# A new list of steps for the first 720 steps of a delta-rule and feed-forward kernel

## The chip, the cores and the metric

One core of a Trainium2 chip runs the whole program. The metric is the device time in microseconds of one execution, the median of several. The engines are PE (TensorE, with PEld for its weight loads), DVE (VectorE), ACT (ScalarE), POOL (GpSimd) and SP (SyncE), which here issues nearly all transfers. Each engine works through its own instructions strictly in the order of the program.

## The reference

A delta-rule recurrence over 768 time steps, for 4 batches of 8 heads of 48 features, and a multiplicative feed-forward network on its output:

```
k_n = k / (norm(k) + 1e-6)
for t in range(S):
    y[t]  = q[t] @ state
    v_old = k_n[t] @ state
    state = state + beta[t] * outer(k_n[t], v[t] - v_old)
x   = y as (3072, 384)
out = (((x @ w1) * (x @ w2)) @ w3) @ w_out
```

w1 and w2 are 384x1024, w3 is 1024x1024, w_out 1024x384, all in float32.

## The kernel before

The 768 time steps are cut into 12 chunks of 64, and two chunks make one of 6 units. Within a chunk the recurrence becomes matrix products with the inverse of a triangular matrix, which is found for a unit (two chunks) at a time in blocks of 32; from chunk to chunk only the state goes on. w3 and w_out are multiplied with each other once (the fold), so that a unit's feed-forward part is two products of 384 by 1024, a multiplication, and one product of 1024 by 384, done with seven half-size products (a Strassen scheme).

Every piece of this is a Python generator, a *part*. A call of `step(name)` runs the part on to its next `yield` and so issues a few instructions. The text ORDER names 1317 steps, one word each; the kernel runs through it once, and `in_text_order()` (L128) then ties each engine to the order in which its instructions were recorded. So ORDER, written out by a planner offline, fixes the order on every engine and of the transfers on SP's queue. Nothing else schedules. A wait of one instruction holds up all that follow on its engine.

The parts that are spoken of below (m is a chunk, j a unit, and a part's steps are told by their place):

- `k`, `q`, `v`: loads of a chunk's keys, queries, values (L202, L213), by SP, those of chunk 0's k and q by ACT. `p`: eight loads of a chunk's keys, then eight of its queries, to be transposed (L230); `d`: DVE's four transposes of these (L324). `K0`, `Q0`, `K1`, `Q1`: the same for chunks 0 and 1 by PE (L337) and copies (L347, L349). `beta`: loads and transposes beta.
- `g`: the squares of the keys on POOL (L270), their sums on DVE (L272), a swap of halves by PE (L255). `N`: norms and weights from these, 15 short instructions on DVE (L279 to L303).
- `s`: a chunk's scores, twice: matmuls (L367, L373), a product on DVE into U (L379), and the masked P, for the first two chunks copied by ACT (L391) and masked by POOL (L393). `u`: four transfers of U to memory (L414).
- `V`: a unit's triangular inverse. POOL clears Vb (L422, L423), SP loads U as blocks (L426), ACT copies Vb to PSUM for the first two units (L434), DVE does 31 elimination steps of two instructions each (L440, L445), ACT copies back (L449), SP stores V (L453).
- `e`: a chunk's corner block: eight loads (L462, L469), a transpose on DVE (L481), matmuls (L498), ACT's copies (L514, L525). `n`: values times norms on POOL (L537).
- `c`: the chain of a chunk: products (L551), differences and scalings on DVE (L584, L594, L613, L615); it ends with the next state.
- `y`: a chunk's outputs: matmuls (L652), eight copies by ACT into xT (L673), and in the third step SP's transfers within xT (L684), six for each of chunks 0 and 1, six for two chunks later.
- `P0` to `P35`: pieces of weights. P0 to P7 are w_out (384 KB as loaded), P8 to P23 are w3 (512 KB), P24 to P29 are w1 and P30 to P35 are w2 (four loads each, 192 and 64 KB in turn). A piece is loaded into one of five raw buffers (L699), split by ACT (L707, L708), masked and joined by DVE (L710, L711), and added by POOL (L715), and only then its raw buffer is free for the load five pieces later.
- `t`: PE's transposes of a w3 piece (L750) and ACT's copy (L753); t0 to t15 belong to P8 to P23. `f`: the fold of a row block (L759, two halves; L766).
- `b`, `a`: unit 0's products with w1 and w2 for chunk 0 (`b`) and chunk 1 (`a0`), later whole units (`a1` and on): L779 on PE, ACT's copy (L791), DVE's multiplication (L795). The first half of each part uses w1, the second w2. They use four PSUM banks in turn.
- `T`, `S`, `o`, `x`: sums of the folded weights (L826), sums of slabs (L846), the seven products (L874), the result (L905 and on) and its transfers (L891).

PE has the same kind of work in every unit once it is under way; the beginning is different, since the weights must be loaded, rebuilt and folded, and the first inverse must be found, before the first product of unit 0 can start.

Of the kernel before, what the change touches and what calls it, by code (L numbers as in the profile page):

```python
# [36 lines left out]


ORDER = """
V0 P0 k0 beta P18 P13 P0 P18 P0 P0 P18 P18 g0 P11 beta P13 K0 K0 P11 P10 q0 P10 P3 k1 P11 P13  # L40
K0 beta P12 g0 P3 K0 g0 K0 g0 P13 K1 g0 P8 P12 g0 K1 K1 P11 P9 Q0 Q0 g0 Q0 P10 P12 g0 Q0 Q0 g0
k2 K1 s0 g0 P9 P10 P8 N0 K1 q1 P2 s0 N0 P3 Q1 s0 P12 p2 g1 Q1 P2 N0 s0 s0 Q1 P9 Q1 P8 Q1 g1 s0
P3 s0 t2 t2 t3 s1 P5 P8 P2 g1 s1 P2 P1 s1 s1 t3 P9 P5 s1 P4 s1 P5 u0 P5 s1 d2 P1 P4 t1 u1 t0 P6
t4 P7 t1 t10 P1 t0 t5 V0 t4 P14 g1 V0 P1 t10 P6 f1 t5 V0 d2 P4 P6 V0 V0 V0 P7 V0 P7 V0 P16 P14
V0 P4 V0 P19 P19 P19 P6 f0 P16 P17 P17 V0 V0 P16 V0 V0 P17 P7 f2 k3 P14 p2 V0 V0 v1 P19 P15 f1
f0 g1 f1 t11 V0 d2 t11 P15 f2 f5 V0 P14 P15 f0 P16 v0 P17 V0 V0 V0 V0 g1 P20 f5 V0 f2 f5 t6 t9
P15 t6 P20 t7 V0 n1 P22 P20 V0 t7 d2 s0 V0 V0 f3 P23 P20 P22 t8 P21 V0 n0 P24 n0 f3 V0 V0 n1 t8
V0 V0 t9 V0 V0 s2 p3 f4 f3 P23 P22 P26 g1 V0 g1 V0 f4 g1 P21 P22 P23 t14 d3 f4 P23 g1 t12 p3 V0
N1 P30 t12 t14 t15 e0 t15 d3 f7 d3 f6 e0 P30 P21 e0 e0 P24 f7 s2 s2 e1 e0 s2 P24 e0 e1 V1 p4 s2
e1 P26 s2 e1 P25 d3 c0 P21 P30 u2 s3 c0 s3 P26 N1 P31 P24 y0 s3 s3 y0 c0 s3 s3 P25 t13 N1 e1 u3  # L50
P31 c0 P26 P31 P32 c1 V1 c1 e1 P25 V1 P27 c1 V1 c1 V1 V1 t13 V1 V1 V1 V1 V1 V1 y0 V1 P25 f7 f6
f6 P30 P32 P32 v2 V1 P27 s1 P31 V1 V1 y1 b3 b1 V1 b0 P32 P28 y1 b1 V1 b1 b3 P29 P27 b2 b3 y1 V1
P27 b1 b0 P29 P29 c1 a01 b2 a03 P28 V1 a01 a00 b3 P28 P29 a02 a02 a03 P35 P28 V1 a05 b7 a00 V1
V1 V1 V1 a06 P33 V1 b5 a05 b7 b0 V1 P34 V1 b5 V1 a06 V1 V1 V1 P34 k4 V1 P35 V1 g2 a00 V1 k5 a00
b0 V1 V1 g2 a04 P34 n2 p4 n2 a07 c1 a04 b2 b4 P33 b6 b2 P35 V1 g2 g2 P34 g2 e2 a07 g2 P33 e2
P35 c2 c2 e3 d4 a03 d4 a03 a01 P33 g2 b4 d4 g2 e2 b6 e2 a07 e2 b4 d4 T a01 T b4 e2 a07 c2 s4 p5
g2 c2 T g2 N2 V2 b6 p5 b6 s4 b5 s4 c2 a06 c2 a06 a04 v3 y2 d5 b5 d5 k6 s4 e3 d5 s4 y2 a02 a05
d5 s4 b7 a04 n3 S0 a02 a05 S0 s5 S0 u4 e3 s5 n3 s5 e3 b7 T o0 c3 c3 s5 g3 s5 S0 N2 N2 x0 e3 g3
e3 o0 s5 c3 c3 u5 o0 x0 V2 S0 x0 y3 V2 y3 S0 V2 S0 V2 S0 S0 V2 V2 V2 S0 g3 o0 S0 o0 S0 x0 V2 c3
o0 v4 y3 V2 V2 V2 x0 p6 V2 x0 V2 S0 a10 a10 S0 g3 S0 x0 V2 x0 S0 o0 x0 x0 p6 a14 V2 k7 a17 a17  # L60
a14 V2 V2 V2 a15 a16 V2 a16 a15 V2 g3 V2 V2 V2 V2 V2 v5 V2 x0 a13 V2 V2 V2 a17 a12 V2 a13 g3 V2
V2 g3 a17 c3 a14 a13 d6 d6 a11 V2 e4 n4 a12 e4 e4 c4 d6 V3 e4 a14 a10 n4 g3 d6 c4 e5 a11 e4 s6
g3 a13 e4 a12 p7 a10 c4 g3 N3 s6 c4 s6 a11 y4 n5 y4 c4 e5 a12 c4 a11 a15 c5 n5 e5 p7 a16 d7 d7
d7 d7 o1 c5 v6 a16 k8 g4 g4 e5 g4 p8 a15 g4 s7 s7 S1 e5 s7 S1 e5 x1 s7 s7 S1 s7 c5 o1 s6 S1 u7
c5 o1 s6 s6 u6 S1 S1 V3 S1 y5 c5 c5 V3 V3 V3 V3 V3 o1 S1 x1 k9 S1 y5 S1 y5 o1 S1 S1 x1 x1 V3 S1
S1 V3 c6 V3 S1 S1 V3 d8 o1 x1 x1 v7 a20 n6 x1 V3 a20 o1 x1 a23 V3 V3 x1 V3 x1 n7 a27 a24 d8 a26
V3 V3 V3 V3 x1 g4 V3 a23 V3 a25 V3 a27 a27 V3 a24 V3 V3 a26 a20 V3 g4 V3 p8 V3 V3 V3 V3 p9 V3
V3 a25 d8 n6 d8 g4 a20 a22 a22 a24 V3 c6 a27 a25 a24 a21 a21 e6 e6 e6 g4 e7 N3 e6 a25 N3 g4 s8
g4 N4 s8 e6 a22 s8 a26 e6 c6 c6 N4 s8 a26 s8 y6 a22 V4 p9 N4 S2 d9 e7 s8 a21 e7 y6 u8 d9 a21 e7
c6 a23 d9 p10 e7 d9 S2 c6 S2 s9 n7 a23 s9 e7 o2 s9 c7 s9 S2 s9 k10 S2 c7 x2 o2 c7 S2 S2 o2 u9  # L70
s9 V4 c7 V4 S2 y7 V4 V4 x2 V4 g5 g5 V4 p10 d10 y7 S2 x2 S2 o2 y7 V4 o2 x2 c7 V4 V4 S2 S2 V4 o2
a35 x2 x2 k11 x2 S2 V4 x2 S2 a35 v8 V4 S2 V4 V4 S2 V4 x2 n8 o2 a37 x2 V4 v9 V4 V4 V4 x2 a34 n8
V4 V4 a36 a30 V4 V4 V4 V4 V4 a37 V4 a34 a33 V4 g5 a33 a30 a32 a36 V4 V4 V4 V4 a34 a33 V4 V5 a32
e8 n9 c7 e8 a30 c8 a33 e8 e9 e8 g5 a35 a34 c8 a30 e8 g5 d10 a32 e9 g5 a32 g5 a36 e8 e9 S3 c8
a36 a35 a31 d10 d10 e9 a31 n9 c8 g5 c8 c8 g5 g5 e9 a31 s10 N5 e9 p11 s10 s10 a31 c9 a37 a37 p11
c9 y8 N5 v11 d11 S3 d11 d11 o3 v10 d11 s10 y8 s10 S3 u10 S3 s11 N5 s11 o3 s10 c9 s11 c9 s11 S3
x3 S3 s11 o3 S3 S3 y9 o3 s11 x3 S3 o3 u11 V5 S3 S3 V5 y9 V5 x3 n11 S3 x3 V5 V5 V5 S3 y9 S3 S3
V5 c9 V5 o3 x3 V5 x3 x3 V5 V5 x3 S3 a47 o3 x3 V5 V5 a47 x3 V5 V5 a47 n10 V5 a46 a40 a40 V5 a47
V5 a43 V5 a46 x3 a42 a45 V5 a42 V5 a41 a45 a43 V5 V5 V5 V5 V5 V5 a44 V5 a44 V5 a45 a41 V5 V5 V5
V5 c9 a42 e10 a40 e10 n11 a42 e10 a44 e10 c10 a45 n10 e11 e10 e11 c10 a43 e10 c10 c10 a40 e11  # L80
a41 a46 e11 c10 a44 S4 a43 e11 a41 S4 c10 o4 e11 a46 c11 x4 S4 S4 y10 o4 c11 c11 S4 y10 S4 S4
S4 S4 S4 c11 o4 y11 o4 x4 S4 S4 S4 o4 y11 x4 x4 o4 S4 x4 x4 S4 y11 S4 x4 x4 a50 x4 o4 a50 x4
a55 a56 a55 a52 a55 a50 a52 a56 a54 a57 a54 a55 a54 a50 a54 a51 a52 a57 a51 a53 x4 a52 a53 a51
a56 a56 a53 a51 a53 a57 o5 S5 a57 S5 S5 o5 S5 S5 S5 x5 S5 S5 S5 o5 o5 x5 S5 S5 S5 o5 S5 S5 S5
o5 x5 S5 x5 o5 x5 x5 x5 x5 x5 x5 x5 x5 x5 x5
"""


# [1 line left out]
def kernel(  # L90
# [36 lines left out]
    def half(z):  # L127
        return slice(C * z, C * z + C)  # L128

    def feat(z):  # L130
        return slice(C * z, C * z + D)
# [6 lines left out]
    def in_turn(pool, shape, tag, n, name, dt=FP32):  # L138

        i = turns.get(tag, -1)  # L140
        while True:
            i = turns[tag] = (i + 1) % n
            if (tag, i) not in held:
                return pool.tile(shape, dt, tag=f"{tag}{i}", name=name, bufs=1)
# [14 lines left out]
    def in_text_order():  # L159
# [15 lines left out]
        out=strict[:], in_=strict[:], pattern=[[1, P]], compare_op=ALU.is_gt,  # L175
# [7 lines left out]
    def padded(name, shape, n, start=0):  # L183
        res = []
        for i in range(n):
            t = persist.tile(shape, FP32, name=f"{name}{i}")
            pool.memset(t[:, start:] if start else t[:], 0.0)
            res.append(t)
        return res

    TTs = padded("TT", [P, NR, H, C], 2)
# [3 lines left out]
    ktoks, vtoks, KQs, PTs, Xs, Ss = {}, {}, {}, {}, {}, {}  # L195
# [114 lines left out]
    def scale_of(x, m, crossed=0):  # L310
        j, cc = divmod(m, 2)
        return x[j][:, cc] if x is ns else x[j][:, crossed, cc]
# [219 lines left out]
    xts = {}  # L532

    def scaled_v(c):
        nv = vtoks[c]
        for r in range(NR):
            pool.tensor_tensor(  # L537
                out=nv[:, r], in0=nv[:, r],
                in1=scale_of(ns, c)[:, r].unsqueeze(2).to_broadcast([P, H, D]), op=ALU.mult,
            )  # L540
            yield

    def chain(c):
        TT, nv, KQ = TTs[c % 2], vtoks[c], KQs[c]

        def products(out, lhs, rhs):
            ps = two_banks()
            for r in range(NR):
                for h in range(H):
                    for z in range(2):  # L550
                        pe.matmul(  # L551
                            out(ps, r, h, z), lhsT=lhs(r, h, z), rhs=rhs(r, h, z),
                            start=True, stop=True,
                        )
            return ps[:, :, 0:DM].rearrange("p b (g d) -> p b g d", d=D)
# [15 lines left out]
            return St[feat(h % 2), z, NP * r + h // 2, :]  # L571

        St = Ss.get(c)
        R = nv
        if c > 0:
            ps = products(
                by_tokens_of_features, lambda r, h, z: KQ[feat(h % 2), NR * z + r, h // 2, 0, :], state
            )
            yield
            R = in_turn(work, [P, NR, H, D], "R", 1, "R")  # L580
            v3, r3 = (
                x[:].rearrange("p r (a e) d -> p (r a) e d", e=2) for x in (nv, R)
            )
            dve.tensor_tensor(  # L584
                out=r3, in0=v3, in1=ps.rearrange("p e g d -> p g e d"), op=ALU.subtract
            )
            yield
        ps = products(
            crossed, lambda r, h, z: TT[half(z), r, h, :], lambda r, h, z: R[half(z), r, h, :]
        )  # L590
        yield
        Xs[c] = X = in_turn(work, [P, NR, H, D], "X", 2, "X")
        for e in range(2):
            dve.tensor_tensor(  # L594
                out=X[:].rearrange("p r (a e) d -> p e (r a) d", e=2)[:, e], in0=ps[:, e],
# [449 lines left out]
```

## Time and profile before

| What | us |
|---|---|
| median of 3 runs | 598.36 |
| the three runs | 594.04, 598.36, 599.14 |
| the profiled execution, its own time | 593.18 |
| its span, first to last instruction | 591.5 |
| mean granted TensorE clock in it | 0.976 |
| L779, products with w1 and w2, busy | 128.0 + 131.8 |
| L874, the seven products, busy | 66.3 + 48.0 |
| L440 and L445, elimination on DVE, busy | 44.7 + 46.0 |
| L759, the fold, busy | 45.5 |

A row of the timeline gives the start in us from the span's start, the length, the engine (SPq is SP's queue of transfers), the line, the operation, the tiles as out<-in, how many were merged, and in brackets the idle time of the engine before it with what ended it. A matmul's records are of single passes: a product of 128 rows shows two records for each call. In the slices the digits are tenths.

### The profile page before, as it was taken

The page shows a single profiled execution, that of the slowest core. Times are in us where ns is not written, and L with a number is a line of the kernel's source. Part 1 is how long each engine was busy: PE and PEld are TensorE (multiplying, and loading weights), DVE is VectorE, ACT ScalarE, POOL GpSimd, SP SyncE. Part 2 cuts the span into 40 slices and gives each one's busy share as a digit, 9 for nine tenths or more (in the row PEclk, how much of TensorE's full clock was granted, in tenths as well). Part 3 has the DMA queues.
Part 4 walks back from the last instruction along what each step waited for, and adds up shares of the span by engine and source line. Part 5 has one row for each costly group of instructions (what it writes and reads, how often), then busy time and mean ns, then how long its engine had stood idle before and what let it go on. Part 6 is the DMA issues. An engine that isn't in the chain of part 4 may idle for free.

```text
span 591.5 us, 19063 instructions
## 1 busy us (share of the span) xinstructions
PE 542.2 (92%) x8188; PEld 379.8 (64%) x8188; DVE 363.0 (61%) x828; ACT 159.3 (27%) x333; POOL 176.3 (30%) x223
## 2 busy tenths in 40 slices
PE   2569898778999999999999989999999999999997
PEld 2466555657878874558854669645698446974477
DVE  3897898569986579574796545865746924110012
ACT  4666354363412202121210232112121112311100
POOL 7563542033464601207121034111170000600051
PEclk9988999679999999999999999999999999999999
DMA  9989986668856455563553345614432040010001
GB/s 245 196 174 267 199 172 130 120 154 169 140 86 98 98 86 111 78 96 54 124 92 79 46 70 103 127 53 66 59 65 90 13 90 4 17 41 13 1 0 53
DMA packets 219507, 57.31 MB, mean 97 GB/s; under 512 B 206656, under 2 KB 212800, under 8 KB 219424
## 3 DMA queue, kind: packets, MB, share of 16 engines
q1 hardware_dynamic: 215232, 55.31, 46.9%
q10 hardware_dynamic: 4192, 0.79, 1.0%
q8 instruction: 64, 1.05, 0.8%
q14 instruction: 19, 0.16, 0.1%
HBM read 43.88 MB, written 11.01 MB: 93 GB/s over the span
## 4 chain that ended last, share of the span: by engine, by line
PE 70%; SPq 10%; DMA 9%; DVE 5%; issue 2%; ACT 1%; POOL 1%; DVEq 0%; POOLq 0%; ACTq 0%
PE ps_f L779 38%; PE ps_f L874 19%; DMA raw<-in_moe_w_dram 5%; PE ps_w L551 5%; PE ps_w L652 4%; SPq L230 3%; SPq L699 2%; PE ps_w L498 2%; DMA ktok<-in_k_dram 2%; DVE tb L440 1%; SPq L202 1%; DVE ps_w L445 1%; PE ps_w L367 1%; DMA Ub<-Ud 1%; PE ps_w L373 1%
## 5 line engine op out<-in xcount | busy, mean ns | idle before, releaser
L779 PE MATMUL ps_f<-xT,w2s 128*128 128x512 f32 (+1 forms) x336 | 131.8, 538 | 2.1 <-issue 2.1
L779 PE MATMUL ps_f<-xT,w1s 128*128 128x512 f32 (+1 forms) x336 | 128.0, 532 | 2.0 <-DMA xT<-xT 2.0
L846 POOL TENSOR_TENSOR ab<-ab 128x256 f32<-128x256 f32 x96 | 67.0, 727 | 175.3 <-DVE ab L795 153.6
L779 PEld LDWEIGHTS ps_f<-xT,w1s 128*128 128x128 f32 x336 | 63.3, 190 | 57.6 <-issue 52.2
L779 PEld LDWEIGHTS ps_f<-xT,w2s 128*128 128x128 f32 x336 | 62.0, 190 | 55.1 <-issue 51.9
L791 ACT COPY ab<-ps_f 128x512 f32<-128x512 f32 (+1 forms) x56 | 28.2, 526 | 165.8 <-PE ps_f L779 161.7
L874 PE MATMUL ps_f<-w,ab 128*128 128x192 f32 x376 | 66.3, 330 | 0.0
L874 PEld LDWEIGHTS ps_f<-w,ab 128*128 128x128 f32 x376 | 61.2, 190 | 4.2 <-issue 3.3
L795 DVE TENSOR_TENSOR ab<-ab,ps_f 128x512 f32<-128x512 f32 (+1 forms) x56 | 33.1, 603 | 48.9 <-PE ps_f L779 48.7
L440 DVE TENSOR_TENSOR tb<-Vb,Ub 128x31 f32<-128x31 f32 (+15 forms) x124 | 44.7, 360 | 17.2 <-DMA Ub<-Ud 13.9
L874 PE MATMUL ps_f<-room,ab 128*128 128x192 f32 x272 | 48.0, 330 | 0.8 <-DVE room L905 0.8
L445 DVE TENSOR_TENSOR Vb<-Vb,tb 128x31 f32<-128x31 f32 (+15 forms) x124 | 46.0, 371 | 4.3
L759 PE MATMUL ps_f<-w2s,w3T 128*128 128x384 f32 x128 | 45.5, 511 | 0.0
L874 PEld LDWEIGHTS ps_f<-room,ab 128*128 128x128 f32 x272 | 44.1, 190 | 1.6 <-issue 1.1
L673 ACT COPY xT<-ps_w 48x256 f32<-48x256 f32 x96 | 30.5, 366 | 54.4 <-PE ps_w L652 53.9
L270 POOL TENSOR_TENSOR sq<-ktok 128x384 f32<-128x384 f32 x24 | 20.7, 866 | 70.0 <-DMA ktok<-in_k_dram 39.5
L759 PEld LDWEIGHTS ps_f<-w2s,w3T 128*128 128x128 f32 x128 | 25.1, 202 | 16.5 <-issue 2.3
L537 POOL TENSOR_TENSOR vtok<-vtok,n 128x384 f32<-128x384 f32 x24 | 20.3, 859 | 43.1 <-DMA vtok<-in_v_dram 43.1
L367 PE MATMUL ps_w<-KQ 48*64 48x128 f32 x384 | 29.3, 293 | 1.7 <-DVE PT L397 1.7
L373 PE MATMUL ps_w<-KQ 48*64 48x64 f32 x768 | 30.1, 232 | 0.0
L715 POOL TENSOR_TENSOR w<-w,raw 128x512 uint32<-128x512 uint32 x16 | 20.6, 1294 | 29.0 <-issue 7.3
L373 PEld LDWEIGHTS ps_w<-KQ 48*64 48x64 f32 x768 | 27.2, 146 | 0.1
(109 smaller groups left out, 661.0 us busy)
## 6 DMA issues: line engine op xcount, KB each, us to landing
raw<-in_moe_w_dram SPq DMA_DIRECT2D x16, 512.0 KB, 6.5
vtok<-in_v_dram SPq DMA_DIRECT2D x24, 192.0 KB, 4.5
raw<-in_moe_w_dram SPq DMA_DIRECT2D x24, 192.0 KB, 4.7
out_dram<-osb SPq DMA_DIRECT2D x46, 96.0 KB, 2.0
ktok<-in_k_dram SPq DMA_DIRECT2D x44, 96.0 KB, 3.6
raw<-in_moe_w_out_dram SPq DMA_DIRECT2D x8, 384.0 KB, 4.4
Ud<-U SPq DMA_DIRECT2D x48, 64.0 KB, 2.6
Ub<-Ud SPq DMA_DIRECT2D x6, 512.0 KB, 4.1
```

What stands on the lines that cost most here:

```text
L367: pe.matmul(ps[half(z), 0, n : n + 128], lhsT=x[:, 0, :], rhs=x.rearrange("p j t -> p (j t)"), start=True, stop=True,)
L373: pe.matmul(ps[half(z ^ j), 1, n + C * j : n + C * j + C], lhsT=x[:, 0, :], rhs=x[:, j, :], start=True, stop=True,)
L440: dve.tensor_tensor(out=tv, in0=V[:, 0 : s + 1, s : s + 1].to_broadcast([P, s + 1, n]), in1=U[:, s, s + 1 : BS].unsqueeze(1).to_broadcast( ...
L445: dve.tensor_tensor(out=o, in0=o, in1=tv, op=ALU.subtract)
L551: pe.matmul(out(ps, r, h, z), lhsT=lhs(r, h, z), rhs=rhs(r, h, z), start=True, stop=True,)
L673: act.copy(out=xT[f, p:NP:2, b : b + NR, cc, :].rearrange("p a r t -> p r a t"), in_=pyv[f, z, b : b + NR],)
L759: pe.matmul(ps[:, 0:DM], lhsT=w3Ts[jc, kc // 4][:, kc % 4 * P : kc % 4 * P + P], rhs=wo[:, kc], start=(kc == 0), stop=(kc == KF - 1),)
L779: pe.matmul(ps[:].rearrange("p b c t -> p b (c t)"), lhsT=w[:, m, js], rhs=x[:, m, :, c0:c1].rearrange("p b c t -> p b (c t)"), start=(m = ...
L791: act.copy(out=t, in_=ps)
L795: dve.tensor_tensor(out=t, in0=t, in1=ps, op=ALU.mult)
L846: pool.tensor_tensor(out=o_, in0=x_, in1=y_, op=op)
L874: pe.matmul(ps[b][:, b, :], lhsT=abs_[u, HF * f + i][:, t0 : t0 + P], rhs=ws_[w][:, i], start=first and i == 0 and (b == 0 or n == "F"), s ...
```

## The change

The first 720 words of ORDER are replaced by another arrangement of the same 720 words; each part keeps its own steps in their order, and the 597 words behind them are as they were. The planner that made the list was given longer times for the fetching of instructions. In two parts a look-up is moved: `vtoks[c]`, the tile of a chunk's values, is now looked up where it is used and no longer at the part's first step, so that `c4` can begin in the list before `v4` is issued. Instructions and their operands are the same. Line numbers behind L535 are one smaller after the change.

The beginning of both lists, up to the load of U for the first inverse (the second `V0`), and the core of the rest of the diff:

```diff
 ORDER = """
-V0 P0 k0 beta P18 P13 P0 P18 P0 P0 P18 P18 g0 P11 beta P13 K0 K0 P11 P10 q0 P10 P3 k1 P11 P13
-K0 beta P12 g0 P3 K0 g0 K0 g0 P13 K1 g0 P8 P12 g0 K1 K1 P11 P9 Q0 Q0 g0 Q0 P10 P12 g0 Q0 Q0 g0
-k2 K1 s0 g0 P9 P10 P8 N0 K1 q1 P2 s0 N0 P3 Q1 s0 P12 p2 g1 Q1 P2 N0 s0 s0 Q1 P9 Q1 P8 Q1 g1 s0
-P3 s0 t2 t2 t3 s1 P5 P8 P2 g1 s1 P2 P1 s1 s1 t3 P9 P5 s1 P4 s1 P5 u0 P5 s1 d2 P1 P4 t1 u1 t0 P6
-t4 P7 t1 t10 P1 t0 t5 V0 t4 P14 g1 V0 P1 t10 P6 f1 t5 V0 d2 P4 P6 V0 V0 V0 P7 V0 P7 V0 P16 P14
...
+P12 k0 beta P2 P0 P11 P12 P2 P12 P12 beta beta g0 K0 g0 P9 P0 t4 P3 k1 P0 P2 K0 P2 K0 P11 K0 q0
+g0 t4 P10 K1 P11 g0 g0 g0 g0 g0 q1 K0 P9 P11 P0 K1 g0 P1 K1 K1 K1 k2 P10 g0 P3 P9 P9 Q0 P10 Q0
+P3 t1 Q0 Q0 Q1 Q0 Q1 Q1 t1 P1 s0 Q1 Q1 N0 P3 P10 P8 P1 s0 p2 g1 s0 s1 s0 s1 g1 P5 g1 P1 P13 s1
+g1 s0 P8 s0 V0 t2 P8 P8 s1 s1 s1 t2 s0 P5 P4 P7 u0 t0 P13 N0 P13 t3 P4 N0 P5 t0 P7 u1 P6 P5 d2
+P18 P7 t3 V0 V0 P6 V0 P4 P6 P18 d2 V0 V0 V0 V0 k3 V0 P18 V0 V0 f1 f0 V0 f2 P7 P4 v0 P6 f1 f0
...
     def scaled_v(c):
-        nv = vtoks[c]
         for r in range(NR):
             pool.tensor_tensor(
-                out=nv[:, r], in0=nv[:, r],
+                out=vtoks[c][:, r], in0=vtoks[c][:, r],
...
     def chain(c):
-        TT, nv, KQ = TTs[c % 2], vtoks[c], KQs[c]
+        TT, KQ = TTs[c % 2], KQs[c]
...
-        R = nv
+        R = vtoks.get(c)
...
-                x[:].rearrange("p r (a e) d -> p (r a) e d", e=2) for x in (nv, R)
+                x[:].rearrange("p r (a e) d -> p (r a) e d", e=2) for x in (vtoks[c], R)
```

The order of the weight pieces' loads on SP, in which each waits for the piece five places ahead of it:

```
before: P0 P18 P13 P11 P10 P3 P12 P8 P9 P2 P5 P1 P4 P6 P7 | P14 P16 P19 P17 P15 P20 P22 P23 P21 P24 P26 | P30 P25 P31 P32 | P27 P28 P29 P35 P33 P34
after:  P12 P2 P0 P11 P9 P3 P10 P1 P8 P5 P13 P4 P7 P6 P18 | P17 P14 P19 P16 P15 P20 P22 P23 P24 P21 P25 | P31 P26 P28 P30 | P32 P29 P27 P34 P35 P33
```

The bars stand at V0's load of U, V0's store, and V1's load of U. Other moves that are spoken of below: before V0's load, k2 stands behind q1 and P1 (before: ahead of q1), and the load of P18 stands right before V0's load (before: that of P7). After V0's load come k3 and v0, then the five w3 pieces, and only then the eight loads of p2's queries (before: four w3 pieces, k3, those eight loads, v1, P15, v0). On ACT, the last copy of e1 (L525) has the piece P28 ahead of it (before: P31). v2's loads stand behind y1's transfers (before: ahead of P28). On POOL, P30's add stands behind P32's (before: far ahead).

## The prediction

> **What bounds the kernel now.** I read the busy table and the slices first, then the span cut into five stretches, then the chain of waits, then the timelines of SP, PE and ACT between 100 and 160 us. The lists of steps part for their first 720 entries; the last 597 are the same.
>
> ```profile
> PE 542.2 (92%) x8188; PEld 379.8 (64%) x8188; DVE 363.0 (61%) x828; ACT 159.3 (27%) x333; POOL 176.3 (30%) x223
> ...
> PE   2569898778999999999999989999999999999997
> ...
> PEclk9988999679999999999999999999999999999999
> DMA  9989986668856455563553345614432040010001
> ...
> q8 instruction: 64, 1.05, 0.8%
> ```
>
> PE is the bound, but only after a beginning: its idle time lies in the first ten slices (14.8 us each). There the DMA engines are nearly full at first, and the granted clock has a hole in slices 8 and 9. The stretches put numbers to it.
>
> ```profile
> 0.00:45.00 45.00, 22.44 (x487) 19.93 (x488) 31.00 (x59) 26.08 (x46) 28.47 (x40) 0.96 0.95 203
> 45.00:90.00 45.00, 41.38 (x193) 25.88 (x192) 37.96 (x98) 23.01 (x44) 20.27 (x19) 0.93 0.92 214
> 90.00:142.00 52.00, 39.86 (x990) 30.98 (x989) 36.35 (x84) 24.30 (x52) 12.53 (x11) 0.84 0.67 134
> 142.00:300.00 158.00, 155.02 (x2740) 118.35 (x2739) 115.64 (x269) 35.35 (x82) 55.61 (x71) 1.00 0.57 101
> ```
>
> The columns after the length are PE, PEld, DVE, ACT and POOL busy, granted clock, DMA share, GB/s. PE is idle 22.6 us before 45, 3.6 to 90, 12.1 to 142, and only 3.0 in the next 158. So all that a new list can change is the moment at which PE becomes full (about 142), and the stalls it might put behind that. PE's work before that moment is the same: up to the first product of unit 0 (L779) both lists give PE 1564 matmul records. What counts is when that product may start and whether it then runs on. The timelines say who decides: first SP, then PE, then ACT.
>
> ```profile
> 109.92 3.71 SPq L414 DMA_DIRECT2D Ud<-U  x4
> ...
> 121.11 0.34 SPq L426 DMA_DIRECT2D Ub<-Ud  x1
> 121.50 1.83 SPq L699 DMA_DIRECT2D raw<-in_moe_w_dram  x4
> 123.43 5.71 SPq L684 DMA_DIRECT2D xT<-xT  x6
> 129.23 2.00 SPq L213 DMA_DIRECT2D vtok<-in_v_dram  x2
> 131.33 4.02 SPq L699 DMA_DIRECT2D raw<-in_moe_w_dram  x8
> 135.87 4.82 SPq L684 DMA_DIRECT2D xT<-xT  x6
> ```
>
> ```profile
> 122.41 2.08 PE L551 MATMUL ps_w<-R,TT 64*64 64x48 f32 x64 [3.78 <-ACT TT L525]
> ...
> 131.96 3.26 PE L779 MATMUL ps_f<-xT,w1s 128*128 128x256 f32 x14 [0.42 <-DMA xT<-xT]
> ...
> 141.59 10.60 PE L779 MATMUL ps_f<-xT,w1s 128*128 128x256 f32 x48 [1.63 <-DMA xT<-xT]
> ```
>
> ```profile
> 108.93 2.58 ACT L673 COPY xT<-ps_w 48x256 f32<-48x256 f32 x8 [4.55 <-PE ps_w L652]
> ...
> 119.48 0.66 ACT L707 ACTIVATE w2s<-raw 128x512 f32<-128x512 f32 x1 [4.27 <-DMA raw<-in_moe_w_dram]
> 120.04 0.67 ACT L708 ACTIVATE raw<-raw 128x512 uint32<-128x512 uint32 x1
> 120.73 1.20 ACT L525 ACTIVATE TT<-ps_w 32x512 f32<-32x512 f32 x2
> ```
>
> Chunk 0's outputs were copied by 111.5 (108.93 + 2.58), but their transfers went out from 123.43: they stood in SP's queue behind work issued back to back. PE's two short waits for xT (0.42, 1.63) are waits for that queue. ACT and PE have a stall of their own (3.78), since the copy L525 stood behind a weight piece that landed late; but by 131.96 PE stands before xT all the same. **SP's queue paces the beginning.**
>
> **The change part by part.** The sum is made against the profiled execution: 593.18 us, a span of 591.5 and 1.7 around it. It lies 5.2 under the median 598.36 of the three runs shown; I carry the difference over to the median.
>
> *Counts on SP, milestone by milestone.* Place of the transfer in SP's queue, before and after: V0's load of U is 44th and 44th; V0's store 94th and 94th; e1's last load 114th and 114th; V1's load 143rd and 143rd; y0's transfers 148th to 153rd in both; V1's store 198th and 198th; e2's last load 206th and 206th. In front of each stand as many weight pieces of the same size, with other numbers. Only y1's six move: 164 to 169 become 162 to 167, as v2's two loads (2.00 us) go behind them. So the count alone gives 0 up to y0 and -2.0 at y1.
>
> *Up to V0's load (44.86 before).* P3's load, and k1's behind it, wait for POOL's add of P12 (512 KB) where it was P0's (384 KB), but Vb's two memsets (1.1) no longer stand on POOL ahead of it: about +0.3. k1 is then in for the squares at 18.5 (18.16 before). POOL goes on with two squares (0.8 each), P11 (1.3), P0 (1.0): 22.4. P1's load waits for that, so k2 goes out at 22.6 (20.63 before), 2 us later; but q1's pair, 3.9 us of SP, is already out, and p2's eight loads start at 25.9, not 29.13. N0 on DVE starts at 25.4 (26.05). s0's and s1's matmuls stand behind Q1 on PE and end near 30.5 and 34; s0's masks on POOL end at 34.3 (33.0), P1's add at 36.2; P7's load waits for it, so u0 starts at 36.7 (37.87) and u1 at 39.0. P18's load, newly ahead of V0's, waits for POOL's add of P5: s1's last product (38.4), P13 and N0 and P5 on DVE, the add to 43.3. V0's load goes at 43.8: -1.1. All these are estimates from the rows' durations, good to 2 us.
>
> *V0's elimination on DVE.* Its first product was at 50.77, after an idle 2.35 for ACT's half of P6, which now lands earlier: 48.8. The DVE steps between first and last take 30.8 before and 33.0 after (one weight piece and a reduction more); the 1.9 that DVE waited for P15, whose load stood behind eight loads of p2 and now stands ahead of them, goes. End: 48.8 + 33.0 + 0.5 of gaps = 82.3 against 84.0: -1.7. But the store waits for SP as well (88.24, right after p3's loads ended at 88.15), which has 49 transfers to issue between load and store in both: I take -1.2, between -1.1 (SP) and -1.7 (DVE).
>
> *V0's store to V1's load.* 49 issues in 32.9 us, 0.67 each, the same number after: 0. V1's load at 119.9. *V1 on DVE*: 27.1 becomes 26.2, but the store stood at 158.5 for SP while DVE and ACT were done at 156.8: 0 of the 0.9 counts. e2 comes 1.2 earlier, and PE has products to fill with.
>
> *y0, y1 and the first products.* y0's xT is in at 130.8 instead of 132: -1.2. y1's xT, 3.2 earlier, is there when PE reaches it: the idle 1.63 goes. Against that the second products of b now need P30's add, which POOL does after P32's; near 135 by the rows, 1 before PE comes; the slabs' copies on ACT stand behind P29 and P27, +0.4. Moved T, S0, c4, a1 lie at PE's full stretch, with 3.0 idle in 158 us as it is: 0 (between -1 and +2).
>
> Sum: -1.2 - 1.6 + 0.4 = -2.4. 593.18 becomes 590.8; on the median **596.0**.
>
> *Instruction fetch.* The page has 64 packets on the instruction queue, and PE with PEld 16,376 instructions: one fetch for 256. In the waits up to 170 us PE has 2.9 us of "issue" (1.4 once before L652, 1.0 in two before L551, 0.5 before L750), all where short matmuls follow each other. They can go, or double: -2.9 to +2.9, but before 130 they lie in front of SP's transfers, so I take 0.
>
> The Trainium skill, "Runtime: NRT & Kernel Launch", Instruction fetch mechanics, says that crossing a 16 KiB block is mostly hidden. That speaks against a list made for longer fetches: by it the whole allowance is worth 0. The row (1.4 for one) shows one that is not hidden; were all of the 2.9 saved at the end, the sum would be -5.3.
>
> **The rivals.**
> 1. *More reaches the end.* After, ACT has P28 ahead of e1's last copy, loaded at places 127 to 130, not P31 at 131 to 134; c1's second product could then run near 117.5 instead of 122.41, -4.9, and 598.4 - 2.4 - 4.9 = 591.1. For it: the 3.78 and the granted clock of 0.50 in the three stretches of 5 us from 110 to 125, which made PE's work there slower. Against: y0's transfers wait 12 us on SP regardless.
> 2. *Slower: P18's load holds V0's.* It is new in SP's queue ahead of V0's load and waits for a raw buffer, through P5's add on POOL, P5 and N0 on DVE and t0 on PE. In the before P17's load waited so until 51.84 for P6's add. If P18's is held as long, V0's load goes at 52, 7 later, and everything behind it: 605. It decides from an add of P5 after 45 on, and passes 1% at 51. Against: my estimate is 43.3.
> 3. *Nothing reaches the end*: DMA share 0.95 and 0.92 up to 90 us with the same bytes in front of each milestone; V0 ends as before, and a new stall eats y1's gain: 598.4.
> That the text does not do what it says I exclude: both lists hold each step equally often.
>
> **How the numbers follow.** Likeliest (-2.4) 0.45, rival 1 0.23, rival 2 0.20, rival 3 0.12. About 1% (6 us) is what a measurement of this kernel can tell from no change. Faster by more than that, under 592.4: most of rival 1 and the lower edge of the likeliest, 0.27. Slower, over 604.3: rival 2, 0.20. The rest 0.53. Low end: rival 1 with the 2.9 of fetches, 588; high end: rival 2, 605. The likeliest one's own range is 593 to 600.
>
> **What would show it.** Right: V0's load near 43.8, its store near 87, V1's load near 120, first L779 near 129, no wait for xT near 140, e2's loads about 1 earlier, and as much PE time idle after 142 as before. V0's load after 47, or over 5 us of PE idle between 142 and 300, makes the forecast wrong to the slow side; first products at 125 or earlier, to the fast side.

## The result, and the profile after

The change made the kernel a little slower: 597.66 us (median of 12 runs, 595.50 to 599.67) against 595.65 (12 runs, 590.62 to 599.14). The medians alone part by 2.0 us (0.34%), the means by 2.7 (0.45%); the ratio is given as 1.0057 with a 95% interval of 1.0034 to 1.0079, or 2.0 to 4.7 us. A ratio here and below counts fast runs alone, so that of the twelve runs of e10, e11 and e16 one, one and two slow ones are left out (with them the ratios of the means would be 1.0054, 0.9959 and 0.9999). The profiled execution took 597.82, its span is 596.1, 4.6 more than before's; what is read from this pair of profiles is of single executions.

The busy table and the slices of after:

```profile
PE 549.9 (92%) x8188; PEld 383.8 (64%) x8188; DVE 359.8 (60%) x828; ACT 159.2 (27%) x333; POOL 176.4 (30%) x223
...
PE   3689697789989999999999999999999999999997
...
PEclk9959798769998999999999999999999999999999
```

The same matmul records take 549.9 us of PE instead of 542.2. Beside the hole that before had in slices 8 and 9, PEclk has dips in slices 3, 5 and 13. The stretches say which of them matters (the columns are those of the prediction: PE, PEld, DVE, ACT, POOL busy, granted clock, DMA share, GB/s):

```profile
0.00:45.00 45.00, 28.01 (x496) 22.84 (x497) 30.18 (x61) 26.71 (x48) 27.06 (x40) 0.85 0.94 202
45.00:90.00 45.00, 37.81 (x179) 23.24 (x179) 37.22 (x97) 21.79 (x41) 21.39 (x20) 0.92 0.91 203
90.00:142.00 52.00, 42.77 (x996) 33.13 (x995) 36.56 (x83) 25.06 (x53) 12.43 (x12) 0.80 0.66 142
142.00:300.00 158.00, 153.29 (x2724) 117.07 (x2723) 110.53 (x261) 35.07 (x81) 54.20 (x68) 0.99 0.58 100
```

Up to 142 us PE has done 1671 records here and 1670 in before: level, whatever the clock was. Between 142 and 300 it does 2724 instead of 2740, is idle 4.7 us instead of 3.0, and the clock is 0.99. What PE waited for in that stretch (engine, line, releaser: us in total, times, longest):

```profile
PE ps_w L651 <- issue: 1.5, 1, 1.5
PE ps_w L498 <- DVE T L481: 1.3, 1, 1.3
```

The first is new and lies in y2, at 180.3 us. The second is e2's wait for the inverse of unit 1; it is 0.9 in before. Around the first, three windows:

```profile
176.00:178.60 2.60, 2.48 (x183) 2.34 (x172) 2.59 (x6) 0.00 (x0) 1.02 (x2) 1.00 0.74 93
178.60:180.30 1.70, 0.17 (x10) 0.03 (x2) 1.46 (x8) 0.00 (x0) 0.00 (x0) 1.00 0.66 77
180.30:184.00 3.70, 3.69 (x13) 2.99 (x13) 2.35 (x11) 2.54 (x8) 0.00 (x0) 0.54 0.71 87
```

183 short matmuls in 2.6 us, then next to nothing for 1.7 us, then 3.7 us at a clock of 0.54. The products that follow, 18 records, take 1.7 us longer than 18 of the same form behind y2 in before (after, then before):

```profile
180.56 5.84 PE L778 MATMUL ps_f<-xT,w2s 128*128 128x256 f32 x18
182.16 4.15 PE L779 MATMUL ps_f<-xT,w2s 128*128 128x256 f32 x18
```

Wait and half clock, 1.5 and 1.7, with 0.4 more at e2's wait, are most of the loss in this pair of profiles: from a01's first product to s7's start PE needs 131.4 us against 127.4 for the same records, 1.7 more of it idle and 2.3 busy, though a01 starts at the same time (141.3 against 141.6).

The beginning, on SP's queue of after:

```profile
122.13 0.34 SPq L426 DMA_DIRECT2D Ub<-Ud  x1
122.52 1.82 SPq L698 DMA_DIRECT2D raw<-in_moe_w_dram  x4
124.44 4.86 SPq L683 DMA_DIRECT2D xT<-xT  x6
```

V1's load goes at 122.13 (121.11 before), y0's xT at 124.44 (123.43): one later each, not one earlier.

### The profile page after: what moved, and what is told of

Its sections match the earlier page's. It is cut to its first block, busy times and chain, and to the rows that moved or that the text cites. A ratio compares the mean times of both kernels' runs of the same rounds, so it can differ in the third digit from the quotient of the medians.

```text
span 596.1 us, 19072 instructions
## 1 busy us (share of the span) xinstructions
PE 549.9 (92%) x8188; PEld 383.8 (64%) x8188; DVE 359.8 (60%) x828; ACT 159.2 (27%) x333; POOL 176.4 (30%) x223
## 4 chain that ended last, share of the span: by engine, by line
PE 74%; SPq 8%; DMA 8%; DVE 3%; issue 2%; ACT 2%; POOL 0%; ACTq 0%; DVEq 0%
PE ps_f L778 40%; PE ps_f L873 17%; PE ps_w L550 5%; PE ps_w L651 4%; DMA raw<-in_moe_w_dram 4%; PE ps_f L758 3%; SPq L230 2%; PE ps_w L498 2%; SPq L202 2%; DMA Vd<-Vb 1%; SPq L414 1%; PE ps_w L367 1%; DMA X<-in_q_dram 1%; DMA Ud<-U 1%; PE ps_w L373 1%
## 5 line engine op out<-in xcount | busy, mean ns | idle before, releaser
L778 PE MATMUL ps_f<-xT,w2s 128*128 128x512 f32 (+1 forms) x336 | 133.5, 544 | 0.0
L778 PEld LDWEIGHTS ps_f<-xT,w2s 128*128 128x128 f32 x336 | 63.5, 194 | 53.8 <-issue 50.2
L758 PE MATMUL ps_f<-w2s,w3T 128*128 128x384 f32 x128 | 49.6, 545 | 1.9 <-ACT w3T L752 1.9
L758 PEld LDWEIGHTS ps_f<-w2s,w3T 128*128 128x128 f32 x128 | 27.0, 218 | 20.7 <-issue 5.7
L373 PE MATMUL ps_w<-KQ 48*64 48x64 f32 x768 | 31.3, 238 | 1.8 <-issue 1.7
```

Source lines behind the costliest of these rows:

```text
L373: pe.matmul(ps[half(z ^ j), 1, n + C * j : n + C * j + C], lhsT=x[:, 0, :], rhs=x[:, j, :], start=True, stop=True,)
L758: pe.matmul(ps[:, 0:DM], lhsT=w3Ts[jc, kc // 4][:, kc % 4 * P : kc % 4 * P + P], rhs=wo[:, kc], start=(kc == 0), stop=(kc == KF - 1),)
L778: pe.matmul(ps[:].rearrange("p b c t -> p b (c t)"), lhsT=w[:, m, js], rhs=x[:, m, :, c0:c1].rearrange("p b c t -> p b (c t)"), start=(m = ...
```

## The experiments

The theory at the outset, **L**: the loss arises late, behind a01's first product, where c2, e2 and y2 stand without products between them. Its rival, **E**: it arises early, where V0 and V1 end later. **S** came after the first runs: it is split. **F** says that PE's instructions come in blocks of 256, and that a block used up too fast leaves PE waiting. **C**, **Q** and **G** are readings of the early part: V1's copies, SP's queue, or something else. All ratios are to before on the same chip, 10 to 12 runs of the experiment against 23 or 35 of before. Line numbers in the experiments' kernels are up to three smaller than in before.

### Halves of the list

```diff
 e1: steps 1-388 of the new list, then the old list's order
 e2: steps 1-386 of the old list, then the new list's order
 e7: steps 1-459 of the new list, then the old list's order
 e8: steps 1-457 of the old list, then the new list's order
```

> The first 388 steps in the new list's order (up to a01's first product), the remaining ones in the old list's order (b0's last step is taken ahead of a00's first, nothing else differs). Theory L (the loss arises in the late part, where c2, e2 and y2 stand together: 1.5 us of issue wait in y2's first transposes, then some 3.4 us at half clock): the time is that of before, a ratio of 0.995 to 1.003, and y2's first transposes last about 2.3 us as in before. Theory E (the loss arises early: V0's elimination ends 1.3 us later, the store 1.6 later, f6's products fall into the half clock): the ratio is 1.004 to 1.008, as with the whole change.

> The complement: the first 386 steps in the old list's order (up to a01's first product), the remaining ones in the new list's order (b3's last step ahead of a02's first). Theory L: as slow as the whole change, a ratio of 1.004 to 1.008, with y2's first transposes at about 4 us and PE at half clock behind them. Theory E: the time of before, 0.997 to 1.003.

> The first 459 steps in the new list's order (up to the first loads of e2), the others in the old list's order. Theory L, with the loss in c2 and y2 behind that place: ratio 0.997 to 1.002. Theory S: 1.001 to 1.005, and the profile shows no issue wait in y2. Theory E: 1.004 to 1.008.

> The complement: the first 457 steps in the old list's order, the others in the new list's order. Theory L: ratio 1.004 to 1.007, with the issue wait of about 1.6 us in y2. Theory S: 1.002 to 1.004 with that wait. Theory E: 0.998 to 1.002.

Measured: e1 1.0030 (0.9999 to 1.0061), e7 1.0024 (0.9995 to 1.0053); e2 1.0025 (0.9993 to 1.0057), e8 1.0018 (0.9993 to 1.0044). The four values lie where S has them, and the pairs multiply to 1.0055 and 1.0042, which is about the whole. But each interval by itself holds 1, so S is the likeliest and not shown by these runs. The later ones with the new beginning and the old rest (e9, e13) also came out above 1, which speaks against L; against E there are only e2 and e8.

The waits of PE between 142 and 300 us in e8 begin with the one of after (e2 has it too, 1.7); in e1 and e7 it is not there, though e7 has 2.2 us of waits for S before 163 and half clock behind them:

```profile
PE ps_w L649 <- issue: 1.5, 1, 1.5
```

### The late half: products moved, short steps moved

```diff
 e3 (new list)
-S0 a06 y2 c2 a07 N2 y2 b5 b6
+S0 a06 a07 b5 y2 c2 N2 y2 b6
 e4 (old list)
-b5 s4 c2 a06 c2 a06 a04 v3 y2 d5
+b5 s4 c2 c2 v3 y2 a06 a06 a04 d5
 e5: e3, and (new list)
-c2 e2 e2 b4 c2
+c2 b4 e2 e2 c2
 e12 (old list)
-b5 s4 c2 a06 c2 a06 a04 v3 y2 d5
+b5 s4 a06 a06 a04 c2 c2 v3 y2 d5
```

> The new list with two second products, a07's and b5's, taken from behind y2's first step to ahead of it, so that two products of 1.5 us stand between c2's last matmuls and y2, as in the old list. Theory L: the issue wait in y2 (1.54 us) and the half clock behind it go, and the ratio to before falls from 1.006 to between 0.999 and 1.002. Theory E: nothing changes, 1.004 to 1.008.

> The old list with the two second products of a06 and a04 taken from ahead of y2's first step to behind it, so that y2 follows c2's last matmuls at once. Theory L: a wait of 1 to 1.5 us in y2 and half clock behind it appear in the kernel before, ratio 1.003 to 1.006. Theory E: no difference, 0.998 to 1.002.

> The new list with a07's and b5's second products ahead of y2's first step and b4's second product between c2's first matmuls and e2's corner products, where PE waited 1.3 us after a01's product in the new list. Theory L (late waits and the half clock behind them carry the loss): ratio 0.998 to 1.001. Theory S (the loss is split: about 1.4 us arises before a01's first product and about 1.8 behind it, as the first two experiments put it): ratio 1.001 to 1.004. Theory E (early alone): 1.004 to 1.008.

> The old list with the second products of a06 and a04 ahead of c2's last matmuls instead of behind them, so that c2's 64 and y2's first 128 matmuls follow each other, as in the new list; no other step moves. Theory F: a block of 256 instructions is used up there in about 2.3 us, an issue wait of 1.3 to 1.7 us appears in y2, ratio 1.002 to 1.004. If issue waits at this place cost nothing in the end: 0.999 to 1.001.

Measured: e3 1.0038 (1.0013 to 1.0063), e5 1.0035 (1.0010 to 1.0059), e4 1.0017 (0.9988 to 1.0046), e12 0.9988 (0.9962 to 1.0013). In e3 the wait in y2 is gone, and e2's wait heads its list:

```profile
PE ps_w L496 <- DVE T L479: 1.5, 1, 1.5
```

So two products do take the wait away; that any of the loss comes back with it is not shown, as the intervals of e3 and of the whole change (1.0034 to 1.0079) overlap. The profile of e3 shows why it need not bring much. Its half clock now stands behind e2's wait, and from a01 to s7 PE needs 131.1 us, as long as in after (e5, without half clock there, 129.0; e1 127.4):

```profile
164.00:166.00 2.00, 1.43 (x66) 1.31 (x67) 1.71 (x3) 0.53 (x1) 2.00 (x3) 0.76 0.51 81
166.00:168.00 2.00, 2.00 (x6) 1.30 (x4) 0.00 (x0) 0.63 (x2) 1.23 (x3) 0.50 0.71 114
```

e4 answers nothing: y2, brought forward, met a wait of its own, 1.9 us for PT from DVE (L395 there), with half clock behind it (0.63 and 0.52 in the two stretches of 2 us from 174). e12 is a miss: c2 and y2 stand together, and no issue wait comes in y2. The block of 256 instructions that ends in y2 was used in 1.84 us, less than the 2.36 of after, but the block in front of it had taken 7.5 us; in e8 it had taken 3.5. That the next block was already there is a reading, not shown.

### The wait at 345 us

```diff
 e6 (old list)
-e7 c6 a23 d9
+e7 a23 c6 d9
 e15: e6 with a23's last step and o2's first product brought forward
-e7 c6 a23 d9 p10 e7 d9 S2 c6 S2 s9 n7 a23 s9 e7 o2
+e7 a23 c6 d9 p10 e7 d9 S2 a23 c6 S2 o2 s9 n7 s9 e7
```

> The old list with one step of the part that both lists share moved by one place: a23's second product goes ahead of c6's last matmuls. Until now e7's and c6's 128 short matmuls and their 128 weight loads, 256 instructions, run in 1.55 us, and an issue wait of 1.1 to 2.05 us follows at instruction 10177 in every profile so far. Theory F (PE's instructions come in blocks of 256 fetched one ahead, and a block that is used up in less than the 3.6 to 3.9 us of a fetch leaves PE waiting for the rest): with 2.7 us of product inside that block the wait goes, ratio 0.9965 to 0.9985. Theory W (the wait belongs to the step a23, for example to its bank or its weights): it stays in front of a23's product, ratio 0.999 to 1.001.

> The old list with the other half of the faster version alone: a23's second product ahead of c6's last matmuls and o2's first product ahead of s9's scores. Theory F: no issue wait near 345, 0.9965 to 0.9985. If the gain of the faster version was all in k5's move: 0.9995 to 1.001.

Measured: e6 1.0009 (0.9987 to 1.0031), e15 0.9997 (0.9969 to 1.0025). The longest wait of PE between 330 and 360 us, in before, e6 and e15:

```profile
PE ps_f L779 <- issue: 2.1, 1, 2.1
```

```profile
PE ps_w L365 <- DVE S L613: 1.5, 1, 1.5
```

```profile
PE ps_w L365 <- DVE PT L395: 0.6, 1, 0.6
```

F is right about the wait and wrong about the gain. The 2.7 us product inside the block removes it (W falls: a23's product is the same), but in e6 PE then meets s9 before c6's bank is free and waits 1.5, with some 1.7 lost to half clock in o2 behind it (0.74, 0.50 and 0.91 in the three stretches of 2 us from 346). With o2 ahead of s9 that goes too, and e15's profile has 1.0 of a new wait near 446; its ratio shows no gain.

### The early half: V1's chain

In the six profiles with the old beginning (before, e2, e4, e6, e8, e12) and the seven with the new one (after, e1, e3, e5, e7, e9, e10) the mean times in us are:

| | old | new |
|---|---|---|
| V0's load of U | 45.5 | 44.4 |
| V0's store | 88.0 | 88.5 |
| V1's load of U | 119.8 | 120.5 |
| V1's second copy on ACT | 121.0 | 125.6 |
| V1's first elimination | 125.4 | 126.9 |
| V1's store | 157.3 | 158.5 |
| e2's corner products | 164.7 | 166.5 |
| a01's first product | 139.9 | 140.0 |

PE comes to a01 at the same time, but what it waits for next, unit 1's inverse, is 1.8 later. Single profiles of one kind lie up to 6 us apart at these places (e2's products at 161.6 to 167.6 in the old, 164.6 to 167.7 in the new), so of the rows only the copies, 4.6 later, stand well clear of that. Two causes could be seen: the copies, and V1's store, which stands on SP behind k5's and p4's loads (2.6 us behind ACT in the new, 1.6 in the old). On before's ACT, then after's ACT and SP:

```profile
121.96 1.21 ACT L434 COPY ps_w<-Vb 128x512 f32<-128x512 f32 x2
```

```profile
124.21 0.68 ACT L706 ACTIVATE w2s<-raw 128x512 f32<-128x512 f32 x1 [2.32 <-DMA raw<-in_moe_w_dram]
124.80 0.66 ACT L707 ACTIVATE raw<-raw 128x512 uint32<-128x512 uint32 x1
125.35 1.21 ACT L434 COPY ps_w<-Vb 128x512 f32<-128x512 f32 x2
```

```profile
155.34 4.34 SPq L230 DMA_DIRECT2D qperm<-in_q_dram  x8
159.78 0.43 SPq L453 DMA_DIRECT2D Vd<-Vb  x1
```

In after ACT waits for P30's piece, and V1's copies stand behind that.

```diff
 e9: e1 with V1's fill and copies moved
-e0 p4
+e0 V1 p4
-c1 P30 c1 P26 V1 c1 V1 f6 P32 V1 N1 c1 V1
+c1 P30 c1 c1 V1 V1 V1 P26 f6 P32 N1 c1
 e10: the new list with this and e5's moves
 e13: e1 with k5's load moved
-k5 a00 ... P35 V1 g2 g2 P34 g2 e2 a07 g2 ... P33 g2
+a00 ... P35 V1 k5 g2 g2 P34 e2 a07 ... P33 g2 g2 g2
 e14: the old list with k5's load moved
 e11: e14 and e15 together
 e16: the new list with k5's load moved, e3's and e15's moves
 e17: e13 and e15, V1's fill as in e9, and V1's copies ahead of P30
-e0 p4
+e0 V1 p4
-c1 P30 c1 P26 V1 c1 V1 f6 P32 V1 N1 c1 V1
+c1 c1 P26 c1 V1 V1 V1 P30 f6 P32 N1 c1
 e18: e11 and e12 together
```

> The first experiment (new list up to a01's first product, old list behind it), with three steps moved: V1's fill on POOL goes to where the old list has it, ahead of p4, and V1's two copies on ACT go ahead of P26's step on ACT. In the profiles of the new beginning ACT stood 2.3 to 5.0 us before that weight piece, so that the copies began 3.2 to 6.0 us after V1's load was issued (0.3 to 0.9 in the old one) and V1's first elimination 5.4 to 7.2 us after it (5.3 to 6.2). Theory C (these copies are what the new beginning costs, by way of the time at which e2's loads can start): the copies begin within 1 us of the load, the first elimination 5.3 to 6.0 us behind it, and the ratio falls from 1.0024 to 1.0030, as the two kernels with the new beginning and the old rest had it, to 0.999 to 1.0015. Theory G (the beginning costs something else, such as the longer half clock there): 1.002 to 1.004.

> The new list with all three repairs: V1's fill and copies as in the run before, two second products ahead of y2, one ahead of e2's corner products. Theory C with L (V1's copies, the wait before e2 and the issue wait in y2 together are the loss): 0.999 to 1.002, against 1.0035 with the last two repairs alone. Theory G: 1.003 to 1.0045.

> The first experiment again (new list up to a01's first product, old list behind it), with k5's load moved from ahead of p4's loads to behind V1's store on SP, and k5's two squares on POOL three places later. In the seven profiles with the new beginning V1's store was issued 1.3 to 3.4 us after ACT had its data ready (mean 2.6; 1.6 in the six with the old beginning), and e2's corner products began 1.8 us later (166.5 against 164.7). Theory Q (SP's queue in front of V1's store and e2's loads passes the cost of the new beginning on): the store waits under 0.5, e2's products start near 165, ratio 0.998 to 1.001 against 1.0024 to 1.0051 for the three kernels with this beginning so far. Theory G (something else in the beginning): 1.002 to 1.004.

> The old list with that move alone. Theory Q: V1's store right behind ACT, PE's wait before e2's corner products (0.9) gone, ratio 0.997 to 0.999. If e2's start is no bound in the old list: 0.9995 to 1.001.

> An attempt at a version better than both. The old list, with k5's load moved from ahead of p4's eight loads to behind V1's store, where SP stood idle 2.6 us (the two squares of k5 on POOL three places later); and with a23's second product ahead of c6's last matmuls and o2's first product ahead of s9's scores, which waited 1.5 us for c6's bank in the sixth experiment. V1's store should go out 1.5 us earlier and the 0.9 us of PE's wait before e2 go; the 2.05 us of issue wait near 345 us should go without a wait in its place: ratio 0.994 to 0.997 if PE is the bound up to the end, 0.998 to 1.001 if another wait takes the time back as in the sixth experiment.

> The whole new list with k5's load behind V1's store, a07's and b5's second products ahead of y2, and the two moves near 345. Theory Q with F: 0.996 to 1.000, against 1.006 for the new list as it is. Theory G: 1.001 to 1.003, as far above the improved old list (0.995) as the new list is above the old one.

> New list up to a01's first product and old list behind it, with k5's load behind V1's store and the two moves near 345 us (as in the faster version of the old list, 0.9949), and now with V1's fill early and its two copies on ACT ahead of P30's step, the one that ACT really stood at (2.2 to 5.2 us for its load in six profiles; the repair of e9 had moved P26's, which is on DVE, and the copies still began 5.3 us behind the load). Theory C with Q (V1's chain carries the cost of the new beginning): copies within 1 us of V1's load, e2's products near 164, ratio 0.994 to 0.997. Theory G: 0.9975 to 1.000, the same 0.2 to 0.3% above the old beginning as without repairs.

> The improved old list (k5's load behind V1's store, the moves near 345) with the second products of a06 and a04 ahead of c2's last matmuls too (0.9988 by itself). If the gains stand: 0.993 to 0.996. If the first figure of the improved list was partly luck, as its halves (1.0007 and 0.9997) suggest: 0.997 to 0.999.

| run | ratio | 95% interval |
|---|---|---|
| e9 | 1.0051 | 1.0027 to 1.0076 |
| e10 | 1.0043 | 1.0016 to 1.0070 |
| e13 | 1.0022 | 0.9991 to 1.0054 |
| e14 | 1.0007 | 0.9978 to 1.0036 |
| e11 | 0.9949 | 0.9924 to 0.9975 |
| e16 | 0.9978 | 0.9944 to 1.0012 |
| e17 | 0.9962 | 0.9939 to 0.9984 |
| e18 | 0.9974 | 0.9946 to 1.0002 |

e9 and e10 tested nothing early: P26's step is DVE's, ACT stood at P30's, and the copies still began 5.7 and 4.1 us after the start of V1's load. e13 freed the store (0.0 behind ACT) but not the copies, which began 5.8 us after that start and held the first elimination to 128.8; e2's products came at 166.1, and the ratio hardly moved: nothing shows that Q alone is enough. In e17 both are free. ACT and SP of e17:

```profile
118.99 1.21 ACT L432 COPY ps_w<-Vb 128x512 f32<-128x512 f32 x2 [0.28 <-DVE R L581]
122.21 0.67 ACT L704 ACTIVATE w2s<-raw 128x512 f32<-128x512 f32 x1 [2.01 <-DMA raw<-in_moe_w_dram]
```

```profile
149.91 5.17 SPq L228 DMA_DIRECT2D qperm<-in_q_dram  x8
155.18 0.43 SPq L451 DMA_DIRECT2D Vd<-Vb  x1
155.71 2.69 SPq L200 DMA_DIRECT2D ktok<-in_k_dram  x4
158.50 2.16 SPq L460 DMA_DIRECT2D TT<-Vd  x4
```

The copies start with the load (118.97), the store goes at 155.18, k5's load fills the gap up to e2's loads, and e2's products start at 163.1, as early as in e11 (163.7). e17's ratio, 0.9962, lies between those on the old beginning with k5's move and the tail's, those near 345 us (e11 0.9949, e18 0.9974). So with V1's chain mended no cost of the new beginning can be seen any more, where e1, e7, e9 and e13 had 0.2 to 0.5%. That is what C with Q forecast, and it is the best reading, but it is not shown alone. The move of the copies was never run without the tail's moves. The same k5 and tail moves took 0.5% from the old list (e14 and e15 together, e11), so most of the 0.7% between e1 and e17 may be theirs. e16 came to 0.9978 although its copies still began 5.3 us after V1's load. And e17's interval reaches into the range that G had (0.9975 to 1.000).

The traces hold a form of G that no run tested, the granted clock. Between 130 and 580 us half clock came in stretches of 3.4 us (6.8 where two met): in five of the ten profiles with the old beginning, 1.7 us in the mean, and in nine of the ten with the new, 5.1 us in the mean; e17 is the one without. At full load 3.4 us of half clock lose 1.7, so the difference of 3.4 is worth about 1.7 us, or 0.3%, as much as the early half cost. In after, e3, e7 and e9 such a stretch follows a wait behind a01, so it may be the way in which the waits cost; whether the new beginning brings it in another way too stays open.

e11 and e17 came out faster than before, each with its whole interval below 1. How the gain of e11 divides stays open: its halves, e14 and e15, gave 1.0007 and 0.9997. Either they help only together (e14's profile still has the 1.5 us wait near 345, e15's store still goes out 1.2 us behind ACT), or e11 and its halves were lucky and unlucky; e18 puts the improved list nearer 0.997.

## Why the prediction was wrong

It said 596.0 against 598.4, a gain of 2.4 us; the runs show a loss of 2.0 to 4.7. That 597.66 is still near 596.0 is luck: the median of the three runs of before that the number was built on lay 2.7 above that of all twelve. By its own steps:

- *V0's load, -1.1*: borne out in the means over the profiles, -1.2; in after's own profile, which the sum was made for, it went at 44.55, only 0.3 earlier and not at 43.8.
- *V0's elimination, -1.7*: wrong. The first product was to start at 48.8; it started at 50.73, since the load that went out at 44.5 had still to land. DVE of after:

```profile
50.73 0.19 DVE L440 TENSOR_TENSOR tb<-ps_w,Ub 128x31 f32<-128x31 f32 x1 [1.88 <-DMA Ub<-Ud]
```

  In before ACT's copy was the last to come, so moving the other steps forward only showed the load behind it. It ended at 85.3 instead of 82.3, since the elimination itself also took 34.6 and not 33.5.
- *V0's store, -1.2, and "49 issues in 32.9 us ... the same number after: 0"*: the count held (32.2 us), the start did not: store +1.6, V1's load +1.0.
- *V1, "0 of the 0.9 counts. e2 comes 1.2 earlier"*: this is the step that failed early. e2's loads came 1.4 later, 163.04 against 161.60. Its working had V1 as DVE time and SP places, and no term for V1's fill and copies, which the new list puts 45 and 8 places later, behind a weight piece on ACT. How much of the early loss goes through this step is not settled (above).
- *y1's xT, "the idle 1.63 goes"*: right, it went. But the first products began at 132.4, not 129, so a01 gained 0.2, and PE then stood before e2.
- *"Moved T, S0, c4, a1 lie at PE's full stretch ...: 0 (between -1 and +2)"*: this is the term that was mis-sized. It measured +4.0 in the pair of profiles: 1.5 of issue wait, about 1.7 of half clock behind it, 0.4 at e2, and the rest in small pieces. The reason given, that PE lies at full stretch there, is what made a new wait and a slower clock cost their whole length.
- *"Instruction fetch: ... I take 0"*: right for the waits before 130: they grew to 4.8 us (2.9 in before), and PE was level at 142 all the same. But they were counted where before had them; the new list made one where PE has nothing to spare.

Rival 3, that nothing reaches the end and a new stall eats y1's gain, is what happened, with the stall larger than the gain. Rival 2 did not come: P18's load went at 43.4. Nor did rival 1: e1's last copy did run earlier (118.8 against 120.7), but c1's second product came at 123.4, behind a wait for S, an issue wait and half clock, and not at 117.5. The sign that was named, over 5 us of PE idle between 142 and 300, was just missed (4.7), as half the loss was clock and not idle time.

## What to carry to other kernels

When a list is rearranged under a full engine, the dependent chain that feeds its next wait (here V1's copies, store and reload) has to be followed instruction by instruction on every queue: counts of transfers hid a copy that had come to stand behind a late piece. A stall taken away is worth what the next wait leaves of it, as the 2.1 us at 345 showed, which brought nothing by itself. And a wait in a full stretch costs about twice where the clock drops behind it (1.5 and 1.7 us in y2).

## What the runs showed of the hardware

Issue waits sit at block borders. Count PE's matmuls, weight loads, semaphore and drain instructions in order of their start, in all 20 profiles of this study: of 86 waits of over 0.25 us that the profile calls issue, 84 end at an instruction whose number is 193 or 194 above a multiple of 256, in whatever step it lies (y2 in after, a23 in before). The other two, 1.2 us each, lie near 122 us in after and e7. How many borders had such a wait, by the time from the start of the first to the end of the last instruction of the block before it:

| stretch, us | under 3 us | 3 to 4 us | over 4 us |
|---|---|---|---|
| 95 to 130 | 20 of 20 | 28 of 37 | 8 of 82 |
| 130 to 300 | 7 of 18 | 0 of 37 | 2 of 404 |
| 300 to 400 | 14 of 14 | 0 of 1 | 0 of 191 |
| 400 to 600 | 4 of 30 | 0 of 40 | 1 of 306 |

The Trainium skill, "Runtime: NRT & Kernel Launch", Instruction fetch mechanics, describes refills of 256 instructions and calls the crossing mostly hidden. The rows agree with the block, and with "mostly" where a block lasts over 4 us (11 waits in 983); under 3 us 45 of 82 are not hidden. The waits last 0.3 to 2.1 us each.

One wait can cost the clock. In after an idle 1.7 us was followed by half clock up to 184.0; in e2 and e8 a wait as long, at the same place, was not, and in e16 one of 0.5 us was (183.5 to 186.9). So the length of the wait alone does not decide it.

The mean granted clock of a run, compared across kernels, told little of the time here: 0.964 to 0.970 over the runs of each kernel with the new beginning, e17 among them, and 0.977 to 0.980 with the old one. In after's profile the largest part of the difference lies before 45 us (0.85 against 0.96), where PE is idle over a third of the time.
